# A causal window attention and a token/channel MLP mixer on one core: another planner table, transposed sums stored as they are, and softmax, u and stores planned apart

## The chip, the cores and the metric

The kernel runs on one core of a Trainium2 chip. The metric is the device time of one launch in microseconds (us). Beside it stands one execution that the hardware profiler recorded: its span, and what each engine did in it. Engines are called PE (matrix multiply; PEld is its weight load), DVE (vector), ACT (scalar), POOL and SP (the last two mostly issue transfers here).

## The reference

x is 8 batches of 4096 rows of 192 values, in float32. First each row becomes a weighted sum of itself and the six rows before it, with weights from a softmax over 7 taps for each of 8 heads of 24 values. Then an MLP over the rows of a batch (token mixing, 4096 to 256 to 4096) is added, and then an MLP over the values (channel mixing, 192 to 1536 to 192).

```
w = exp(wg - max(wg));  w = w / (sum(w) + 1e-9)                 # over the 7 taps
x[b, s, h] = sum over k of w[b, s, h, k] * x_pad[b, s + k, h]   # 24 values a head
u = x + (relu(x.T @ w_tok1) @ w_tok2).T                         # per batch, over 4096 rows
out = u + relu(u @ w_ch1) @ w_ch2
```

## The kernel before

The 32,768 rows are cut into 64 **chunks** of 512 rows (8 to a batch); chunk and group numbers below are the same 0 to 63. Products that must be near float32 are made as two or three fast matmuls on a high and a low part, so nearly every tile has a `_hi` and a `_lo` twin that ACT (cast) and DVE (subtraction) make.

The stages of a chunk:

- **attention**: for each tap k, DVE multiplies the chunk's rows by the weights (`product`, L203). Tap 0 goes to the sum `xa`; taps 1 to 6 each go to a buffer `pr` (4 of them) and are added to `xa` by a transfer that accumulates (L221, issued on POOL). The next addition to the same `xa` waits until the last has landed, and a `pr` buffer is free when its addition has landed. Chunks go in **pairs**, tap by tap: product for one, product for the other, and so on, so 12 additions a pair;
- **turn** (L285): DVE transposes `xa` in blocks of 32 by 32, ACT moves 24 blocks into place (L293), and two transfers on ACT's queue keep the result `xs` in DRAM (L275, L276). It comes back later as `xb` (L313, L314, on SP's queue);
- **token1** (L483, L484; `th`): PE multiplies `xa` by the first token weights and DVE adds the result to `h1s`. From the third batch on it takes `xh`, the high and low parts of `xa` (L257 on ACT, L260 on DVE). When all 8 chunks of a batch are through, `make_h1` gives `h1`;
- **token2** (L513; `up`): PE multiplies `h1` by the second token weights for chunk m; DVE adds `xb` (L520 to L522) and gives u; ACT and DVE make its parts (L524 to L529). token2 of a batch's first chunk needs `h1` of that batch, so the last token1 of the batch before it;
- **channel1** (`ph`, L544, L549) and **channel2** (`acc`, L567): for each group three rounds q = 0, 1, 2. channel1 of a round fills two `ph` tiles, ACT and DVE turn each into `h` (L552, L553), and channel2 of the round before follows on PE. A round's channel1 and channel2 together are called a **slot** here;
- **store**: DVE adds `acc` to u (L577 to L579), which also frees the only `acc` tile, and transposes twice (L581, L582); ACT moves 12 blocks (L589) into `out_tile`, and two transfers on ACT's queue write them out (L599).

A prologue makes chunks 0 to 7 (the first batch) in another way, on PE, and turns the int64-boxed weights into float32 (`convert`).

**The order.** Every engine takes its instructions in the order of the program, and the program's order is made by a planner written out in the kernel: PE's order is a loop over groups and rounds, in which one token1 or token2 fits after each slot. All other work stands in chains of items with a cost, and `pump` issues items, earliest start first, while they end before a limit. `at` holds the planned time of each engine. An item is "v" (DVE), "a", "s" or "u" (ACT), "n" or "t" (no cost; "t" only once its wait is over), "gate" (a condition) or "w" (a time to wait for). How long an addition takes to land is a constant of the plan:

```
ISSUE, ADD = 1000, 5000          # L606, ns
done[m] = on("pool", ISSUE, at["dve"] + HOP, done.get(m, 0.0)) + ADD     # L223
pr_free.append(done[m])                                                   # L224
yield "w", 0, lambda: pr_free.popleft()                                   # L232, ahead of a product
```

Nothing of the plan is checked at run time: an engine that comes to a product whose buffer is not free stands there, with all that follows it in its order. `need` (L697) is what the loop calls where PE cannot go on: it moves the planned time of PE on by 500 ns at a time until the condition holds.

Of the kernel before, what the change touches and what calls it, by code (L numbers as in the profile page):

```python
# [21 lines left out]
def mixer_kernel(ctx: ExitStack, tc: tile.TileContext, x, wg, wt1, wt2, wc1, wc2, out):  # L22
# [22 lines left out]
    TAPS = [(k,) for k in range(K)]  # L45
    PR = 4

# [115 lines left out]
    def softmax(m):  # L163
        t = wgt.pop(m)
        nt = SM * CT
        wn = p1.tile([P, K, nt, H], F32, tag="wn", name="wn")
# [4 lines left out]
        yield "v", 540, lambda: nc.vector.tensor_reduce(mx, t, axis=AX.X, op=ALU.max)  # L171
        yield "v", 540, lambda: nc.vector.tensor_sub(t, t, bc(mx))
        yield "a", 470, lambda: nc.scalar.activation(t, t, AF.Exp)
        yield "v", 540, lambda: nc.vector.tensor_reduce(mx, t, axis=AX.X, op=ALU.add)
# [5 lines left out]
        yield "v", 540, lambda: nc.vector.tensor_mul(wn.rearrange("p k t h -> p t h k"), t, bc(mx))  # L180
# [15 lines left out]
    def attention(ms):  # L196

        done, sums = {}, {}
        cost = 70 + CT * D * 1.05
# [8 lines left out]
        def one(m, k, first):  # L208
            t = new_xa(m) if k == 0 else late.tile([P, CT, D], F32, tag="pr", name="pr", bufs=PR)
            product(m, k, t)  # L210
            if first:
                sums[m] = t
            else:
                prt[m] = t

        def add_dve(m):
            nc.vector.tensor_add(sums[m], sums[m], prt.pop(m))
            pr_free.append(at["dve"])
# [7 lines left out]
        for ks in TAPS:  # L226
            for m in ms:
                for k in ks:
                    if k == 0:
                        yield "gate", 0, lambda m=m: xa_free(m)  # L230
                    else:
                        yield "w", 0, lambda: pr_free.popleft()  # L232
                    yield "v", cost, lambda m=m, k=k: one(m, k, k == ks[0])
                    if k != ks[0]:
                        yield "v", cost, lambda m=m: add_dve(m)
                if ks[0] != 0:
                    yield "n", 0, lambda m=m: add_dma(m)

        def summed(m):
            xa_at[m] = done[m]  # L240
            add_chain(two_parts(m), done[m])
            state["summed"] = m
        for m in ms:
# [7 lines left out]
    def two_parts(m):  # L251
# [9 lines left out]
        if m // NCH >= F1:  # L261
            yield "a", 760, hi
            yield "v", 876, lo
# [6 lines left out]
    Q = 32  # L270

    def keep(m, t):

        xst[m] = dram.tile([2, P, N], F32, name=f"xs{m}")
        nc.scalar.dma_start(xst[m][0], t[:, 0, :])  # L275
        nc.scalar.dma_start(xst[m][1, DC:P], t[DC:P, 1, :])  # L276

    def turns():

        for m in range(NCH, NG):  # L280
            box = {}

            def turn():
                box["t"] = late.tile([P, CT, D], F32, tag="t", name="t")
                nc.vector.transpose(box["t"].rearrange("p c d -> p (c d)"), xat[m].rearrange("p c d -> p (c d)"))  # L285
                box["s"] = late.tile([P, 2, N], F32, tag="ts", name="ts")
                state["turned"] = m

            def move(part):
                t = box["t"].rearrange("p c (d j) -> p c d j", j=Q)  # L290
                for d, n in part:
                    dst, to = (box["s"][:, 0], d * Q) if d < DA // Q else (box["s"][:, 1], DC + d * Q - DA)
                    nc.scalar.copy(dst[to:to + Q, :].rearrange("p (c n j) -> p c n j", c=CT, j=Q)[:, :, n, :],  # L293
                                   t[n * Q:(n + 1) * Q, :, d, :])
            yield "gate", 0, lambda: state["summed"] >= m
            yield "w", 0, lambda: xa_at[m]
            yield "v", 876, turn
            every = [(d, n) for d in range(D // Q) for n in range(P // Q)]
            for at_ in range(0, len(every), MOVES):
                part = every[at_:at_ + MOVES]  # L300
                yield "u", 300 * len(part), lambda part=part: move(part)

            def last():
                keep(m, box["s"])
                state["kept"] = m
                return max(at["act"], at["pe"]) + KEEP
            yield "w", 0, last

    def load_xt(m):

        xbt[m] = p1.tile([P, 2, N], F32, tag="xb", name="xb", bufs=2)
        s = xst.pop(m)
        nc.sync.dma_start(xbt[m][:, 0, :], s[0])  # L313
        nc.sync.dma_start(xbt[m][DC:P, 1, :], s[1, DC:P])  # L314
# [26 lines left out]
    def turn_first(m):  # L341
# [9 lines left out]
        nc.scalar.copy(t[:, 0, :], ps[:, 0, :])  # L351
        nc.scalar.copy(t[DC:P, 1, :], ps[DC:P, 1, :])
        if m >= 2:
            keep(m, t)
# [40 lines left out]
    def convert_w2(i):  # L395
# [5 lines left out]
        v = v.rearrange("p (k n c) -> p k n c", k=KR, c=CT)  # L401
        t = p1.tile([P, KR, 2, N], F32R, tag="w2", name="w2")
        hi, lo = (t[:, :, l].rearrange("p k (c n) -> p k n c", c=CT) for l in range(2))
# [3 lines left out]
        def last():  # L407
            state["vals"] -= 1
            w2t[i] = t
            nc.gpsimd.dma_start(s3[i], t.rearrange("p k l n -> p (k l n)").bitcast(F32))  # L410
        yield "n", 0, last

    def load_w2(m):
        t = p1.tile([P, KR, 2, N], F32R, tag="w2", name="w2")
        nc.sync.dma_start(t.rearrange("p k l n -> p (k l n)").bitcast(F32), s3[m % NCH])
# [90 lines left out]
    def token2(m):  # L506
# [3 lines left out]
        for n, steps in ((1, ((C_HL, 0), (C_HL, 1))), (0, ((A_HI, 0), (A_HI, 1), (A_LO, 0)))):  # L510
            for k in range(KR):
                for j, (d, l) in enumerate(steps):
                    nc.tensor.matmul(up[:, n, :], h1[:, k, d], w[:, k, l, :], start=k == 0 and j == 0,  # L513
# [5 lines left out]
        c = slice(0, DC)  # L519
        nc.vector.tensor_add(uc[c], up[DC:P, 1, :], xb[DC:P, 1, :])  # L520
        nc.vector.tensor_add(uc[c], up[c, 1, :], uc[c])
        nc.vector.tensor_add(ua, up[:, 0, :], xb[:, 0, :])  # L522
        a_hi, a_lo, c_hi, c_lo = (late.tile([P, N], F32R, tag=x, name=x, bufs=2) for x in ("a_hi", "a_lo", "c_hi", "c_lo"))
        nc.scalar.copy(c_hi[c], uc[c])  # L524
# [431 lines left out]
```

## Time and profile before

| what | value |
|---|---|
| time, 3 runs | 2341.88 us median (2335.44 to 2349.58) |
| profiled execution | 2351.83 us, span 2350.1 us |
| PE busy | 2188.0 us (93%) |
| DVE busy | 1624.9 us (69%) |
| ACT busy | 1405.7 us (60%), of it 397.5 us for the 1344 moves of L293 |
| POOL busy | 304.4 us, 336 additions issued |
| transfers | 429.65 MB, mean 183 GB/s |

How to read the rows: a group of instructions has busy time and mean duration, then the idle time of its engine just before them and what ended it. A row of waits has total us, how often, and the longest. In a timeline row the bracket holds the idle time ahead of the instruction and what ended it. A row of stretches gives busy time and count of each engine in a stretch, then the clock granted to PE (1.00 is full speed), the busy share of the 16 transfer engines, and GB/s. Matmuls overlap, so a PE row's mean duration is longer than the time from one matmul to the next.

### The profile page before, as it was taken

The page shows a single profiled execution, that of the slowest core. Times are in us where ns is not written, and L with a number is a line of the kernel's source. Part 1 is how long each engine was busy: PE and PEld are TensorE (multiplying, and loading weights), DVE is VectorE, ACT ScalarE, POOL GpSimd, SP SyncE. Part 2 cuts the span into 40 slices and gives each one's busy share as a digit, 9 for nine tenths or more (in the row PEclk, how much of TensorE's full clock was granted, in tenths as well). Part 3 has the DMA queues.
Part 4 walks back from the last instruction along what each step waited for, and adds up shares of the span by engine and source line. Part 5 has one row for each costly group of instructions (what it writes and reads, how often), then busy time and mean ns, then how long its engine had stood idle before and what let it go on. Part 6 is the DMA issues. An engine that isn't in the chain of part 4 may idle for free.

```text
span 2350.1 us, 28487 instructions
## 1 busy us (share of the span) xinstructions
PE 2188.0 (93%) x10464; PEld 1703.4 (72%) x10464; DVE 1624.9 (69%) x1932; ACT 1405.7 (60%) x2969; POOL 304.4 (13%) x359
## 2 busy tenths in 40 slices
PE   8968999899899999999999999999999999999998
PEld 5746777677677777777777777777777777777776
DVE  8886888686666767667777776676776667544443
ACT  5546786566666656665556766555666656544444
POOL 0011222111111111111111111111111111000000
PEclk9978999899999999999999999999999999999999
DMA  7677989896778787677887777778777777212210
GB/s 283 221 197 211 247 223 233 215 250 164 214 200 219 203 187 203 168 207 195 199 223 185 186 189 204 194 192 223 172 184 204 192 195 173 93 63 63 63 57 21
DMA packets 131820, 429.65 MB, mean 183 GB/s; under 512 B 16232, under 2 KB 26728, under 8 KB 116320
## 3 DMA queue, kind: packets, MB, share of 16 engines
q0 software_dynamic: 49536, 140.53, 31.6%
q1 hardware_dynamic: 58016, 237.74, 29.8%
q10 hardware_dynamic: 24128, 49.56, 8.0%
q8 instruction: 82, 1.34, 0.2%
q14 instruction: 58, 0.48, 0.1%
HBM read 225.13 MB, written 70.52 MB: 126 GB/s over the span
## 4 chain that ended last, share of the span: by engine, by line
PE 34%; DMA 29%; DVE 17%; ACT 14%; issue 4%; ACTq 1%; SPq 0%; POOLq 0%; DVEq 0%
DMA xa<-pr 24%; PE acc L567 13%; PE ph L544 8%; ACT ts L293 6%; DVE h L553 5%; PE ph L549 4%; ACT out_tile L589 4%; DVE pr L203 3%; PE tapsum L336 3%; PE up L513 2%; ACT h L552 2%; DMA xt<-in_x_dram 2%; DVE t L285 1%; DVE xa L203 1%; DMA val<-s 1%
## 5 line engine op out<-in xcount | busy, mean ns | idle before, releaser
L567 PE MATMUL acc<-h,w2s 128*128 128x512 f32 x3840 | 936.9, 399 | 34.4 <-DVE ua L579 34.3
L567 PEld LDWEIGHTS acc<-h,w2s 128*128 128x128 f32 x3840 | 713.9, 190 | 247.0 <-issue 88.6
L552 ACT ACTIVATE h<-ph 128x1024 fp32r<-128x1024 f32 x384 | 373.2, 1024 | 332.8 <-PE ph L549 312.5
L553 DVE SCALAR_TENSOR_TENSOR h<-ph,h 128x1024 fp32r<-128x1024 f32 x384 | 450.9, 1215 | 171.9 <-ACT h L552 171.9
L221 POOL DMA_DIRECT2D xa<-pr x336 | 292.7, 874 | 1554.7 <-DVE pr L203 806.7
L293 ACT COPY ts<-t 32x128 f32<-32x128 f32 x1344 | 397.5, 296 | 47.8 <-DMA xs<-ts 10.0
L203 DVE TENSOR_TENSOR pr<-xt,wn 128x768 f32<-128x768 f32 x336 | 310.0, 946 | 157.6 <-DMA xa<-pr 156.6
L544 PE MATMUL ph<-a_hi,w1a_hi 128*128 128x512 f32 x768 | 316.2, 412 | 71.7 <-DVE h L553 64.2
L544 PE MATMUL ph<-a_hi,w1a_lo 128*128 128x512 f32 x768 | 310.8, 405 | 0.0
L544 PE MATMUL ph<-a_lo,w1a_hi 128*128 128x512 f32 x768 | 310.5, 404 | 0.1
L544 PEld LDWEIGHTS ph<-a_hi,w1a_hi 128*128 128x128 f32 x768 | 151.2, 197 | 110.6 <-DVE h L553 71.2
L589 ACT COPY out_tile<-ua 32x256 f32<-32x256 f32 x512 | 206.8, 404 | 8.5 <-DVE ua L582 1.8
L513 PE MATMUL up<-w,h 128*128 128x512 f32 x640 | 161.7, 400 | 21.0 <-ACT w L404 10.6
L544 PEld LDWEIGHTS ph<-a_lo,w1a_hi 128*128 128x128 f32 x768 | 151.1, 197 | 34.1 <-DVE a_lo L527 1.2
L544 PEld LDWEIGHTS ph<-a_hi,w1a_lo 128*128 128x128 f32 x768 | 151.5, 197 | 30.1
L549 PE MATMUL ph<-c_hi,w1c_hi 64*128 64x512 f32 x768 | 172.7, 446 | 0.0
L513 PEld LDWEIGHTS up<-w,h 128*128 128x128 f32 x640 | 123.4, 193 | 48.5 <-ACT w L404 11.0
L549 PE MATMUL ph<-c_lo,w1c_hi 64*128 64x512 f32 x768 | 152.3, 393 | 0.0
L549 PE MATMUL ph<-c_hi,w1c_lo 64*128 64x512 f32 x768 | 151.4, 391 | 0.0
L520 DVE TENSOR_TENSOR uc<-up,xb 64x512 f32<-64x512 f32 x64 | 44.4, 693 | 130.7 <-ACT out_tile L589 103.4
L549 PEld LDWEIGHTS ph<-c_hi,w1c_hi 64*128 64x128 f32 x768 | 72.4, 185 | 78.5 <-issue 69.4
L483 PE MATMUL th<-xh,w 128*128 128x384 f32 x384 | 113.7, 360 | 10.5 <-ACT w L157 9.3
(77 smaller groups left out, 1963.4 us busy)
## 6 DMA issues: line engine op xcount, KB each, us to landing
xa<-pr POOLq DMA_DIRECT2D x336, 384.0 KB, 5.9
w<-s SPq DMA_DIRECT2D x96, 1024.0 KB, 6.3
xt<-in_x_dram SPq DMA_DIRECT2D x56, 960.0 KB, 9.2
out_dram<-out_tile ACTq DMA_DIRECT2D x128, 192.0 KB, 3.1
raw<-in_moe_w_tok_dram SPq DMA_DIRECT2D x16, 1024.0 KB, 6.6
xs<-ts ACTq DMA_DIRECT2D x62, 256.0 KB, 5.2
xb<-xs SPq DMA_DIRECT2D x62, 256.0 KB, 7.1
s<-w POOLq DMA_DIRECT2D x8, 1024.0 KB, 9.8
```

What stands on the lines that cost most here:

```text
L203: nc.vector.tensor_mul(t.rearrange("p t (h g) -> p (t h) g", h=H).rearrange("p (o n) g -> p o n g", o=1), x_k, w)
L221: nc.gpsimd.dma_start(xat[m].rearrange("p t d -> p (t d)"), sums[m].rearrange("p t d -> p (t d)"), accum_op=ALU.add)
L293: nc.scalar.copy(dst[to:to + Q, :].rearrange("p (c n j) -> p c n j", c=CT, j=Q)[:, :, n, :], t[n * Q:(n + 1) * Q, :, d, :])
L336: nc.tensor.matmul(ps[:, n, 0:half * D], ident, prs[k][:, n * half:(n + 1) * half, :], start=k == 0, stop=k == K - 1)
L483: nc.tensor.matmul(th[:, r, 0:2 * D], w[:, c, 0, rs], xh[:, c, :], start=c == 0, stop=False)
L513: nc.tensor.matmul(up[:, n, :], h1[:, k, d], w[:, k, l, :], start=k == 0 and j == 0, stop=k == KR - 1 and j == len(steps) - 1)
L544: nc.tensor.matmul(ph[p][:, j, :], w[:, fs], u, start=n == 0, stop=False)
L549: nc.tensor.matmul(ph[p][:, j, :], w[rows, p * P:(p + 1) * P], u[rows], start=False, stop=n == 2)
L552: nc.scalar.activation(h[:, :, 0, :], ph[p], AF.Relu)
L553: nc.vector.scalar_tensor_tensor(h[:, :, 1, :], ph[p], 0.0, h[:, :, 0, :].bitcast(F32), op0=ALU.max, op1=ALU.subtract)
L567: nc.tensor.matmul(acc[:, n, :], w2s[:, f, d], h[:, j, l, :], start=f == 0 and i == 0, stop=f == NF - 1 and i == len(steps) - 1, skip_grou ...
L589: nc.scalar.copy(dst, src[to:to + Q].rearrange("p (c n k d) -> p c n k d", c=CT, n=2, d=Q)[:, :, n])
```

## The change: what it does

**Plan numbers.** ISSUE and ADD go from 1000 and 5000 to 900 and 7000, LOAD (a load's landing) from 5000 to 8000; the costs of the other items move by some per cent. The tap table gets a second form (two taps summed on DVE), used from chunk EARLY * 8 on; EARLY is 8, so from chunk 64, which does not exist. Every pair keeps its 12 additions.

**Turn.** The 24 ACT moves and the two stores on ACT's queue for each of 56 chunks go. DVE's transpose writes its blocks in another order, one transfer on SP's queue stores the tile as it is (128 rows of 3072 bytes), and the load puts the 32-row strips in place with six transfers of 32 rows in pieces of 512 bytes. Columns of u are then in another order, and the second token weights and the last moves follow it.

**Items of their own.** softmax becomes a chain of its own, one pair ahead of the products, with two `wn` tiles. The parts of u are no longer issued with token2 but are items (`u_parts`). The output transfers become "t" items on SP's queue. token2 makes the 128-row half first. `need` may name chains that go first.

```diff
+    TAPS = [(0,), (1, 2), (3, 4), (5, 6)]
+    TAPS0 = [(k,) for k in range(K)]
...
-        for ks in TAPS:
+        for ks in (TAPS if ms[0] >= EARLY * NCH else TAPS0):
...
             def turn():
-                box["t"] = late.tile([P, CT, D], F32, tag="t", name="t")
-                nc.vector.transpose(box["t"].rearrange("p c d -> p (c d)"), xat[m].rearrange("p c d -> p (c d)"))
-                box["s"] = late.tile([P, 2, N], F32, tag="ts", name="ts")
+                t = box["t"] = late.tile([P, D // Q, CT * Q], F32, tag="t", name="t")
+                nc.vector.transpose(t.rearrange("p d (c b) -> p d c b", c=CT),
+                                    xat[m].rearrange("p c (d a) -> p d c a", a=Q))
                 state["turned"] = m
 
-            def move(part):
-                t = box["t"].rearrange("p c (d j) -> p c d j", j=Q)
-                for d, n in part:
...
+            def keep():
+                xst[m] = dram.tile([P, D // Q, CT * Q], F32, name=f"xs{m}")
+                nc.sync.dma_start(xst[m], box["t"])
+                state["kept"] = m
...
+        for d in range(D // Q):
+            dst = t[d * Q:(d + 1) * Q, 0] if d < DA // Q else t[DC + d * Q - DA:DC + (d + 1) * Q - DA, 1]
+            nc.sync.dma_start(dst.rearrange("a (n j) -> a n j", n=P // Q),
+                              s[:, d, :].rearrange("(n a) j -> a n j", a=Q))
...
-        for n, steps in ((1, ((C_HL, 0), (C_HL, 1))), (0, ((A_HI, 0), (A_HI, 1), (A_LO, 0)))):
+        for n, steps in ((0, ((A_HI, 0), (A_HI, 1), (A_LO, 0))), (1, ((C_HL, 0), (C_HL, 1)))):
...
+        yield "u", 620, lambda: nc.scalar.copy(a_hi, ua)
+        yield "u", 620, lambda: nc.scalar.copy(c_hi[c], uc[c])
+        yield "v", 610, lambda: nc.vector.tensor_sub(a_lo, ua, a_hi.bitcast(F32))
+        yield "v", 610, lambda: nc.vector.tensor_sub(c_lo[c], uc[c], c_hi[c].bitcast(F32))
+        yield "u", 620, lambda: nc.scalar.copy(c_hi[e], uc[c])
+        yield "u", 620, lambda: nc.scalar.copy(c_lo[e], c_lo[c].bitcast(F32))
...
-                nc.scalar.dma_start(rows.rearrange("(k p c) d -> p k (c d)", k=OB, c=CT),
+                nc.sync.dma_start(rows.rearrange("(k p c) d -> p k (c d)", k=OB, c=CT),
...
-        yield "n", 0, last
+        yield "n", 0, moved
+        yield "t", 0, last
...
-    ISSUE, ADD = 1000, 5000
+    ISSUE, ADD = 900, 7000
...
-    LOAD = 5000
-    KEEP = 3000
+    LOAD = 8000
...
-    TOP, LOW = 1040, 1235
+    TOP, LOW = 1000, 1180
...
-            for c in chains[2:] + chains[1::-1]:
+            urgent = [c for c in chains if c.key in keys and not c.blocked() and c.item is not None]
+            for c in urgent or chains[3:] + chains[2:0:-1] + chains[:1]:
...
+    def softmaxes():
+
+        for m in range(NCH, NG, SM):
+            yield "gate", 0, lambda: m - SM in soft_at and state["done"] >= m - SM - 1 or m == NCH
+            yield "w", 0, lambda: wg_at.get(m, 0.0)
+            yield from softmax(m)
...
+        soft = softmaxes()
+        run(islice(soft, 2, 9))
         run(w2_it)
...
-                need(token1_ready)
+                need(token1_ready, ("w1", state["token1"] + 1), ("x", state["token1"] + 1))
                 do_token1()
-            need(lambda: g + 1 in w2t and g + 1 in xbt and state["stored"] >= g - 1)
+            need(lambda: g + 1 in w2t and g + 1 in xbt and state["stored"] >= g - 1, (convert_w2, g + 1), ("o", g - 1))
             do_token2(g + 1)
```

**What moves.** DVE in the middle of the program, at the end of a pair's products (`pr`), where `h` is the eviction that PE waits for. Before:

```order
L203 TENSOR_TENSOR pr<-xt,wn 128x768
L553 SCALAR_TENSOR_TENSOR h<-ph,h 128x2x512 x2
L203 TENSOR_TENSOR pr<-xt,wn 128x768 x3
L520 TENSOR_TENSOR uc<-up,xb 64x512
L521 TENSOR_TENSOR uc<-up,uc 64x512
L522 TENSOR_TENSOR ua<-up,xb 128x512
L525 TENSOR_TENSOR c_lo<-uc,c_hi 64x512
L527 TENSOR_TENSOR a_lo<-ua,a_hi 128x512
L203 TENSOR_TENSOR pr<-xt,wn 128x768 x2
L553 SCALAR_TENSOR_TENSOR h<-ph,h 128x2x512 x2
```

and now:

```order
L207 TENSOR_TENSOR pr<-xt,wn 128x768
L589 STREAM_TRANSPOSE ua<-ua 128x512
L207 TENSOR_TENSOR pr<-xt,wn 128x768
L560 SCALAR_TENSOR_TENSOR h<-ph,h 128x2x512 x2
L207 TENSOR_TENSOR pr<-xt,wn 128x768 x2
L175 TENSOR_REDUCE mx<-wg 128x64
L176 TENSOR_TENSOR wg<-wg,mx 128x448
L518 TENSOR_TENSOR ua<-up,xb 128x512
L519 TENSOR_TENSOR uc<-up,xb 64x512
L520 TENSOR_TENSOR uc<-up,uc 64x512
L560 SCALAR_TENSOR_TENSOR h<-ph,h 128x2x512 x2
```

Of a pair's 12 `pr` products the last five stood between two evictions; now two do, and the evictions from the first four products to the last are three instead of two.

ACT in the same part of the program, between evictions (`out_tile` are the moves of the store, `ts` those of the turn). Before:

```order
L552 ACTIVATE h<-ph 128x2x512 x2
L589 COPY out_tile<-uc 32x4x2x32 x2
L589 COPY out_tile<-ua 32x4x2x32 x4
L599 DMA out_dram<-out_tile 32x2x768 x2
L293 COPY ts<-t 32x4x32 x10
L275 DMA xs_8650<-ts 128x512
L276 DMA xs_8650<-ts 64x512
L524 CAST c_hi<-uc 64x512
L526 CAST a_hi<-ua 128x512
L528 CAST c_hi<-uc 64x512
L529 CAST c_lo<-c_lo 64x512
```

and now:

```order
L559 ACTIVATE h<-ph 128x2x512 x2
L596 COPY out_tile<-uc 32x8x32 x2
L596 COPY out_tile<-ua 32x8x32 x4
L559 ACTIVATE h<-ph 128x2x512 x2
L527 CAST a_hi<-ua 128x512
L528 CAST c_hi<-uc 64x512
L531 CAST c_hi<-uc 64x512
L532 CAST c_lo<-c_lo 64x512
L559 ACTIVATE h<-ph 128x2x512 x4
```

No transfer is issued on ACT any more in this part, and the parts of u stand behind an eviction, not before it.

PE where the second batch's first token2 stands. Before:

```order
L549 MATMUL ph<-c_lo,w1c_hi 128x512 x2
L567 MATMUL acc<-h,w2s 128x512 x20
L513 MATMUL up<-w_2772,h_2644 128x512 x10
L544 MATMUL ph<-a_hi,w1a_hi 128x512
L544 MATMUL ph<-a_hi,w1a_lo 128x512
```

and now:

```order
L556 MATMUL ph<-c_lo,w1c_hi 128x512 x2
L574 MATMUL acc<-h,w2s 128x512 x20
L499 MATMUL th<-xa,val 128x192 x16
L511 MATMUL up<-w_2458,h_2794 128x512 x10
L551 MATMUL ph<-a_hi,w1a_hi 128x512
```

Two token1 (8 matmuls each), this token2 and the channel1 that takes its u now follow each other with nothing between; before, the batch's last token1 lay earlier and a slot lay between token2 and its channel1. The third batch's first token2 stands in the same way. Later batches have their last token1 two slots ahead.

More of the change, by code (lines that the diff above doesn't have):

```diff
@@ L681, in pump @@
                     start = max(at["act"], c.wait)
-                    if kind == "s" and scalar or not state["late"] and (start > now + 400 or start + c.item[1] > end):
+                    if kind == "s" and scalar > 1 or not state["late"] and (start > now + 400 or start + c.item[1] > end):
                         continue
@@ L838, in mixer_kernel @@
         pass
+    run(u_parts(0))
+    free["u"] = 0.0
     load_xt(2)
[L840 to L842 removed]
+    att = attentions()
+    run(last)
+    run(c2_it)
+    run(islice(att, FIRST))
+    chains[0:0] = [Chain(att), Chain(turns()), Chain(soft)]
     add_chain(load_w1(NCH))
```

187 lines of the change are left out of this document (93 added, 94 removed).

## The prediction

> **What bounds the kernel now.** I read the page's first parts, then the busy time by stretch, PE's timeline, the waits, and the additions. PE is busy 93% of the span, so it is the engine whose stalls are the time:
>
> ```profile
> PE 2188.0 (93%) x10464; PEld 1703.4 (72%) x10464; DVE 1624.9 (69%) x1932; ACT 1405.7 (60%) x2969; POOL 304.4 (13%) x359
> PEclk9978999899999999999999999999999999999999
> DMA xa<-pr 24%; PE acc L567 13%; PE ph L544 8%; ACT ts L293 6%; DVE h L553 5%; PE ph L549 4%; ACT out_tile L589 4%; DVE pr L203 3%; PE tapsum L336 3%; PE up L513 2%; ACT h L552 2%; DMA xt<-in_x_dram 2%; DVE t L285 1%; DVE xa L203 1%; DMA val<-s 1%
> ```
>
> Yet the chain that ended last runs longest through the landing of additions (24%), and the clock row falls below full speed here and there. How long a group takes when nothing stalls is read from the starts of token2 on PE:
>
> ```profile
> 1723.96 2.43 PE L513 MATMUL up<-w,h 128*128 128x512 f32 x10
> 1755.70 2.43 PE L513 MATMUL up<-w,h 128*128 128x512 f32 x10
> ...
> 1791.61 1.75 PE L513 MATMUL up<-w,h 128*128 128x512 f32 x7
> ...
> 2060.04 1.29 PE L513 MATMUL up<-w,h 128*128 128x512 f32 x5
> ...
> 2089.49 1.75 PE L513 MATMUL up<-w,h 128*128 128x512 f32 x7
> ```
>
> 29.45 us without a token1 (2060.04 to 2089.49), 31.74 with one (1723.96 to 1755.70), so a token1 is 2.29. The group after that took 35.91. Next, the stretches between the first token2, the 17th, the 54th and the end; then the same stretches for token2 (10 matmuls each) and token1 (16 each) alone:
>
> ```profile
> 0.00:124.60 124.60, 109.93 (x480) 78.86 (x480) 105.45 (x84) 67.88 (x85) 3.50 (x10) 1.00 0.75 254
> 124.60:723.00 598.40, 530.55 (x2481) 411.95 (x2482) 458.79 (x551) 390.77 (x833) 105.20 (x124) 0.93 0.83 214
> 723.00:1995.10 1272.10, 1204.93 (x5847) 946.65 (x5846) 898.26 (x1108) 782.51 (x1753) 195.72 (x225) 0.98 0.77 195
> 1995.10:2350.10 355.00, 342.60 (x1659) 265.91 (x1657) 162.45 (x191) 164.53 (x300) 0.00 (x0) 0.99 0.20 60
> ...
> 723.00:1995.10 1272.10, 89.83 (x370) 69.42 (x370) 0.98 0.77 195
> ...
> 124.60:723.00 598.40, 46.34 (x272) 44.12 (x272) 12.64 (x23) 1.42 (x3) 0.93 0.83 214
> 723.00:1995.10 1272.10, 89.29 (x592) 87.49 (x592) 38.60 (x70) 1.92 (x4) 0.98 0.77 195
> ```
>
> Middle: 37 groups, 37 token1, floor 37 x 31.74 = 1174, taken 1272: **98 us lost**. Early: 16 groups and 17 token1, 16 x 29.45 + 17 x 2.29 = 510, less some 14 as the first two groups hold five slots instead of six and one channel2 less: floor about 496, taken 598: **102 us lost**. After 1995 nothing is to be had: groups run at 29.45. So the most that any change of order can bring is some 200 us.
>
> Who makes PE wait in the middle stretch, and who makes those wait:
>
> ```profile
> PE ph L544 <- DVE h L553: 36.0, 14, 3.7
> PE acc L567 <- DVE ua L579: 31.1, 16, 3.6
> DVE pr L203 <- DMA xa<-pr: 137.2, 56, 8.2
> DVE t L285 <- DMA xa<-pr: 48.3, 15, 4.1
> ```
>
> PE waits 67 us, always for DVE; DVE stands 185 us for landings of additions, with evictions behind it. One such place:
>
> ```profile
> 1700.94 0.96 DVE L203 TENSOR_TENSOR pr<-xt,wn 128x768 f32<-128x768 f32 x1 [7.11 <-DMA xa<-pr]
> ...
> 1703.09 0.79 PE L544 MATMUL ph<-a_hi,w1a_hi 128*128 128x512 f32 x1 [2.87 <-DVE h L553]
> ...
> 1703.00:1706.50 3.50, 3.41 (x8) 2.73 (x9) 2.82 (x5) 0.58 (x1) 0.87 (x1) 0.50 0.91 175
> ```
>
> A product stands 7.11 us for a buffer, the eviction behind it is late, PE idles 2.87, and then its clock is 0.50 for the next 3.5 us. So a stall is paid twice; the 98 us are 67 of waiting and about 31 of half clock.
>
> The Trainium skill, "TensorE: Matmul & The Clock Gate", section "HAM oscillation — how this bites in real kernels", gives as its rule that idle gaps over about 3.4 us are to be avoided. By it a gap of 2 to 3 us would cost its own length and no more. The rows differ: 2.87 us were enough for 3.5 us at half clock, so here the measurement decides.
>
> **The change part by part.** *The planned landing.* An addition was planned at 1.0 + 5.0 = 6.0 us from issue to landing, now at 0.9 + 7.0 = 7.9. What it takes:
>
> ```profile
> DMA to landing us min/median/max: 3.9/5.9/13.6
> ...
> 1737.93 1.76 POOL L221 DMA_DIRECT2D xa<-pr  x2 [29.71 <-DVE pr L203]
> 1746.52 0.87 POOL L221 DMA_DIRECT2D xa<-pr  x1 [6.83 <-DMA xa<-pr]
> ...
> 1764.24 0.88 POOL L221 DMA_DIRECT2D xa<-pr  x1 [4.62 <-DMA xa<-pr]
> 1770.12 0.87 POOL L221 DMA_DIRECT2D xa<-pr  x1 [5.00 <-DMA xa<-pr]
> ```
>
> The median is near the old number, but a late one delays all later ones of its chunk. Four rounds took 1764.24 - 1737.93 = 26.3 us, 6.6 each: 2.3 us over the old plan, 5.3 under the new. So DVE, which now meets the product later, finds the buffer free in a pair like this. In the order, three evictions now lie between the first four products and the last two. With a slot at (29.45 - 2.29) / 3 = 9.1 us (11.3 with a token), the last product comes some 34 us after the first, when the fourth round must have landed: 26 to 29 us at 6.6 to 7.3 a round. The turn and the parts of xa come two evictions later, at some 52 us, against 6 x 7 = 42 for the last landing. Slack everywhere, 4 to 10 us; it is gone at 9 us a round. Bounds for the middle stretch: 0 (every wait comes back at another place) and 98 (none does). I take two thirds, **-65**, nearer to none, since 6.6 lies well under 9, but loads collide with single rounds.
>
> What is late next is DVE itself: 898 us in 37 groups is 24.3 us a group of 31.74, so it has 7 us to spare, unevenly: a slot with store, two products for `xa`, turn and parts is fuller than its 11.3 us by about a microsecond, which the token matmul after it covers.
>
> *The turn.* ACT's moves and its transfers:
>
> ```profile
> L293 ACT COPY ts<-t 32x128 f32<-32x128 f32 x1344 | 397.5, 296 | 47.8 <-DMA xs<-ts 10.0
> ...
> 1727.74 0.35 ACTq L275 DMA_DIRECT2D xs<-ts  x1
> 1729.23 0.45 ACTq L276 DMA_DIRECT2D xs<-ts  x1
> 1755.42 0.34 ACTq L599 DMA_DIRECT2D out_dram<-out_tile  x1
> ```
>
> 24 x 0.296 + 0.35 + 0.45 + 2 x 0.34 = 8.6 us of ACT a group go. ACT is busy 782 of 1272, 21 us a group, and PE waits for DVE; so in the middle this is worth nothing by itself. It shortens casts that sit behind moves, and in the early stretch, where weights are converted, it frees ACT: 391 of 598 busy. That is inside the terms. The transpose is one instruction as before.
>
> *The transfers.* The loads become six of 64 KB instead of two:
>
> ```profile
> w<-s SPq DMA_DIRECT2D x96, 1024.0 KB, 6.3
> xs<-ts ACTq DMA_DIRECT2D x62, 256.0 KB, 5.2
> xb<-xs SPq DMA_DIRECT2D x62, 256.0 KB, 7.1
> ...
> SPq L415 <- PE up L513: 1054.9, 52, 25.1
> ```
>
> SP issues per group 1 (turn) + 2 (out) + 4 (more loads) = 7 more, at 0.35 to 0.45 us some 3 us; it already stands 1055 us waiting for token2 alone, so the time is there. The price of 512-byte pieces is not in the trace: from nothing (same bytes) to twice the 7.1 us of today's landing. Behind it, with xb loaded nearly two groups (60 us) ahead, 14 us is still hidden: 0. Should that cover go, DVE would stand before u and the same 2.9 + 1.7 us a stall would be due. The SP wait that is added (a store waits for DVE's transpose or ACT's moves) has the weight loads behind it; token2's next weights have a group's 31.74 us for 6.3.
>
> *The early stretch.* Group 1 begins:
>
> ```profile
> 174.02 0.79 PE L513 MATMUL up<-w,h 128*128 128x512 f32 x1 [10.58 <-ACT w L404]
> ...
> 182.77 0.53 PE L544 MATMUL ph<-a_hi,w1a_hi 128*128 128x512 f32 x1 [2.75 <-ACT a_hi L526]
> ```
>
> PE stands 10.58 us for a converted weight whose conversion lay behind products and another conversion; now it goes first. Bounds 0 and -13.3 (both waits); I take **-10**. Of the 89 us of loss left there, DVE's stands for landings and a crowded ACT make a part; bounds 0 and -89, I take 0.4 of it, **-35**, less than in the middle since conversions stay. Against that, PE's order now has token1, token2 and channel1 in a row at two batch starts. Each pays twice a wait like the 2.75 above (for h1, for u's parts), 5.5, and some 3.5 at half clock, up to 14.5 as group 1 did; I take 10 each, **+20**. The stretch: -25.
>
> *The prologue.* The softmax of the ninth and tenth chunk moves ahead of the first token2: its exponential on ACT and six short DVE operations, bounds 0 and 4 us; **+1**, as ACT takes one more instruction there. The tail after the last matmul is the same.
>
> *The sum*, against the profiled execution's own 2351.83 (span 2350.1, 1.7 around it): -65 - 25 + 1 = **-89**, 2263. That execution was 10 us above the median of the runs, so for the median 2342 - 89 = **2253 us**.
>
> **The rivals.** *The waits move (half).* Loads of 1 MB and two x tiles collide with single rounds, and DVE stands at other products. For it: landings reach 13.6, and the transfer engines are 77% busy and will be busier with shorter groups. Against it: 5.3 us of slack in four rounds. A third of the middle and -6 early: about -39, **2303**.
>
> *Near the floor.* No landing is met late, the half clock goes too, the two batch starts cost little: -90 in the middle, -55 early, +1: **2196**. For it: no other engine is near full. Against it: PE waits in early groups for conversions that remain.
>
> *Slower: additions beyond the plan.* token1 now stands at a fixed place right after its pair's additions, while PE takes nothing else. If a round takes r us, the sixth has landed at 6r, and token1 comes at some 56; from r = 9 PE waits 6 (r - 9) for each of 28 pairs, and 1.7 at half clock. At r = 9.2 that is (1.2 + 1.7) x 28 = +81; the middle's -65 then fails too, and -24 remains of the rest: +57, **2399**. It decides from r = 9 on. For it: single rounds of 8.6 (1737.93 to 1746.52). Against it: the four rounds averaged 6.6.
>
> The Trainium skill, "DMA: Bandwidth & Descriptors", section "Queues, rings and completion order", says that each transfer engine goes round the queue rows that have work, a packet at a time. By it, emptying ACT's row leaves the additions' row a larger turn, not a smaller one, which speaks against this rival; no row here shows the turns, and I give it 0.07 rather than 0.10 for that.
>
> *No change.* The loss goes from landings to DVE's full slots and the two batch starts: **2342**.
>
> **How the numbers follow.** Chances: forecast 0.53, half 0.22, near the floor 0.13, no change 0.05, slower 0.07. What a measurement of this kernel can tell from no change is about 0.5%, 12 us. Faster 0.53 + 0.22 + 0.13 = 0.88, same 0.05, slower 0.07. The range that holds 8 in 10 goes from the near-floor case to just over the half case, 2196 to 2315: it leaves out half of the near-floor case (0.06), no change and slower (0.12). The bounds of the unknown pieces (early -89, middle -98) would reach lower, about 2145, which needs all at once.
>
> **What would show it.** In the changed profile: DVE's stands for landings (185 us in the middle) down to some 60, PE's for h and ua from 67 to some 25; groups in the middle alternating no longer between 31.7 and 36, but near 32.5; the clock there 0.99 or more; a gap of 5 to 15 us on PE at the first token2 of the second and the third batch; ACT's busy time down by 397 us, which by itself moves nothing. It would be wrong if DVE stands as long at turn or parts as it did at products, if a wait for `xb` or token weights shows on PE or DVE, or if token1 waits for `xh`.

## The result, and the profile after

The changed kernel takes **2256.48 us** (median of 4 runs, 2251.6 to 2258.84); the kernel before took 2345.73 beside it. The ratio is 0.961, 95% interval 0.956 to 0.967. Its profiled execution took 2258.16 us (span 2256.3), 93.7 less than the profiled execution before (2351.83). Forecast were 2253 and a difference of 89.

From the page of the changed kernel, the busy times:

```profile
PE 2162.9 (96%) x10464; PEld 1686.6 (75%) x10464; DVE 1618.1 (72%) x1932; ACT 1010.6 (45%) x1625; POOL 300.7 (13%) x359
```

ACT is down by 395 us, and PE by 25, which fits matmuls that no longer run at half clock. The stretches of the prediction, cut again at the first, the 17th and the 54th token2 (columns as in the prediction: length, busy PE, PEld, DVE, ACT, POOL, clock, share of transfer engines, GB/s), and the same for token1 alone (16 matmuls each):

```profile
0.00:125.30 125.30, 109.77 (x480) 78.83 (x480) 108.78 (x90) 68.38 (x86) 3.49 (x10) 1.00 0.76 253
125.30:711.50 586.20, 532.81 (x2509) 413.01 (x2509) 441.53 (x527) 266.54 (x403) 94.66 (x113) 0.95 0.80 203
711.50:1900.60 1189.10, 1175.69 (x5803) 926.51 (x5804) 893.13 (x1112) 521.60 (x873) 192.21 (x224) 0.99 0.86 211
1900.60:2256.30 355.70, 344.62 (x1675) 268.28 (x1673) 174.62 (x207) 154.04 (x264) 10.31 (x12) 0.99 0.30 77
...
125.30:711.50 586.20, 46.22 (x256) 0.95 0.80 203
711.50:1900.60 1189.10, 92.26 (x592) 0.99 0.86 211
```

The floors are made as in the prediction: 29.45 us a group, 2.29 a token1, 14 off in the early stretch. One thing differs: the change has a slot more ahead of the 17th token2 and a slot less behind it. Without token1, PE has 2509 - 256 = 2253 matmuls in the early stretch, where it had 2481 - 272 = 2209, so 44 more; in the middle it has 44 fewer (5803 for 5847, token1 alike); and a slot is 24 matmuls of channel1 and 20 of channel2. At 9.1 us a slot: early, 16 groups, 256/16 = 16 token1 and the slot, floor 503, taken 586, so **83 us lost** (102 before); middle, 37 groups and 592/16 = 37 token1 less the slot, floor 1165, taken 1189, **24 us lost** (98 before). All 24 lie before 950 us; after that every group takes the floor, as two starts of token2 show (PE's timeline):

```profile
1233.98 2.43 PE L511 MATMUL up<-w,h 128*128 128x512 f32 x10
1265.72 2.43 PE L511 MATMUL up<-w,h 128*128 128x512 f32 x10
```

So 74 us came out of the middle and 19 out of the early stretch. Who waits in the middle (711.5 to 1900.6; total, times, longest), DVE first, then PE:

```profile
DVE pr L207 <- DMA xa<-pr: 76.7, 42, 4.1
DVE t L285 <- DMA xs<-t: 14.1, 3, 6.3
...
PE ph L551 <- DVE h L560: 5.2, 2, 5.0
PE th L481 <- DMA w<-s: 3.1, 1, 3.1
PE th L481 <- issue: 2.3, 1, 2.3
PE up L511 <- ACT h L467: 1.8, 1, 1.8
PE ph L551 <- ACT a_hi L527: 1.4, 1, 1.4
```

DVE still stands 77 us at products, but never over 4.1 us (8.2 before), and PE's waits are 15 us in all. After 948 us PE does not wait at all, though most of DVE's stands at products lie there (948.3 to 1900.6):

```profile
DVE pr L207 <- DMA xa<-pr: 60.6, 32, 4.1
```
In the early stretch PE still waits 53 us; the largest:

```profile
PE ph L551 <- ACT a_hi L527: 12.5, 4, 4.3
PE ph L551 <- DVE h L560: 11.6, 2, 6.4
PE th L499 <- DMA val<-s: 11.6, 1, 11.6
PE th L482 <- DVE w L162: 5.0, 1, 5.0
```

The 11.6 us are new. They stand ahead of the second batch's first token2, where the last token1 waits for its weights `val`. PE's timeline, then SP's and DVE's at the same time:

```profile
409.76 2.11 PE L499 MATMUL th<-xa,val 128*128 128x192 f32 x12
423.44 5.46 PE L499 MATMUL th<-xa,val 128*128 128x192 f32 x16 [11.57 <-DMA val<-s]
...
410.50 8.00 SPq L291 DMA_DIRECT2D xs<-t  x2
418.55 0.95 SPq L370 DMA_DIRECT2D val<-s  x2
...
417.17 0.98 DVE L285 STREAM_TRANSPOSE t<-xa 128x768 f32<-128x768 f32 x1 [3.45 <-DMA xs<-t]
```

SP spends 8 us on two stores of transposed sums, the second of which must wait for DVE's transpose; the load of the weights is issued only behind them. The transpose for its part stands 3.45 us for the first store, as there is one tile `t`.

### The profile page after: what moved, and what is told of

Its sections match the earlier page's. It is cut to its first block, busy times and chain, and to the rows that moved or that the text cites. A ratio compares the mean times of both kernels' runs of the same rounds, so it can differ in the third digit from the quotient of the medians.

```text
span 2256.3 us, 27414 instructions
## 1 busy us (share of the span) xinstructions
PE 2162.9 (96%) x10464; PEld 1686.6 (75%) x10464; DVE 1618.1 (72%) x1932; ACT 1010.6 (45%) x1625; POOL 300.7 (13%) x359
## 4 chain that ended last, share of the span: by engine, by line
PE 81%; DMA 8%; DVE 6%; ACT 3%; issue 1%; SPq 0%; POOL 0%; ACTq 0%; DVEq 0%; POOLq 0%
PE acc L574 34%; PE ph L551 20%; PE ph L556 12%; PE up L511 5%; DMA xa<-pr 5%; PE tapsum L331 3%; PE th L481 3%; ACT out_tile L596 1%; PE th L499 1%; PE th L482 1%; DVE h L560 1%; DMA xs<-t 1%; DMA w<-s 1%; ACT h L559 1%; DVE pr L207 1%
## 5 line engine op out<-in xcount | busy, mean ns | idle before, releaser
L574 PE MATMUL acc<-h,w2s 128*128 128x512 f32 x3840 | 926.4, 395 | 2.2 <-DVE ua L586 2.2
L574 PEld LDWEIGHTS acc<-h,w2s 128*128 128x128 f32 x3840 | 706.2, 188 | 210.7 <-issue 68.6
L551 PE MATMUL ph<-a_hi,w1a_hi 128*128 128x512 f32 x768 | 308.0, 401 | 30.7 <-DVE h L560 16.8
L551 PE MATMUL ph<-a_lo,w1a_hi 128*128 128x512 f32 x768 | 305.4, 398 | 2.7 <-DVE a_lo L529 2.6
L551 PE MATMUL ph<-a_hi,w1a_lo 128*128 128x512 f32 x768 | 304.9, 397 | 0.0
L596 ACT COPY out_tile<-uc 32x256 f32<-32x256 f32 x256 | 103.3, 403 | 16.5 <-DVE uc L588 11.9
L482 PE MATMUL th<-xh,w 128*128 128x192 f32 x384 | 98.2, 256 | 5.0 <-DVE w L162 5.0
```

Source lines behind the costliest of these rows:

```text
L482: nc.tensor.matmul(th[:, r, 0:D], w[:, c, 1, rs], xh[:, c, 0:D], start=False, stop=c == CT - 1)
L551: nc.tensor.matmul(ph[p][:, j, :], w[:, fs], u, start=n == 0, stop=False)
L574: nc.tensor.matmul(acc[:, n, :], w2s[:, f, d], h[:, j, l, :], start=f == 0 and i == 0, stop=f == NF - 1 and i == len(steps) - 1, skip_grou ...
L596: nc.scalar.copy(dst, src[to:to + Q].rearrange("p (n e d) -> p n e d", n=2, d=Q)[:, n])
```

## The experiments

Each kernel was timed in three rounds (the last in five) beside the kernel before, which took 2338 to 2348 us in them; ratios are therefore sharper than times. Losses are from each profiled execution, with the floors above, and with its own token1: 16 early (17 in the kernel before, 18 in e3), 36 to 39 in the middle. e1, e3, e5 and e11 have their slots as the kernel before, the others as the change.

| kernel | us | ratio to before (95%) | lost early | lost in the middle |
|---|---|---|---|---|
| before | 2346 | 1 | 102 | 98 |
| the change | 2256 | 0.961 (0.956-0.967) | 83 | 24 |
| e1 change, old landing | 2375 | 1.012 (1.009-1.014) | 105 | 104 |
| e2 landing alone (7.9) | 2229 | 0.949 (0.945-0.952) | 65 | 11 |
| e3 turn alone | 2420 | 1.029 (1.026-1.033) | 98 | 172 |
| e4 change, val ahead | 2248 | 0.957 (0.953-0.960) | 76 | 18 |
| e5 turn and landing | 2239 | 0.958 (0.955-0.960) | 78 | 13 |
| e6 landing 6.9 | 2283 | 0.977 (0.974-0.980) | 94 | 38 |
| e7 landing, conversions earlier | 2246 | 0.961 (0.959-0.963) | 89 | 6 |
| e8 landing 8.9 | 2304 | 0.986 (0.983-0.989) | 118 | 36 |
| e9 change, weights timed | 2255 | 0.962 (0.957-0.967) | 67 | 35 |
| e10 e9, val ahead, early 6.9 | 2242 | 0.956 (0.951-0.960) | 52 | 40 |
| e11 e5 with big loads | 2237 | 0.953 (0.949-0.958) | 75 | 12 |
| e12 e10, two t tiles | 2207 | 0.941 (0.938-0.944) | 45 | 11 |

**e1 and e2: the landing taken out, and the landing alone.** The same line, in the changed kernel and in the kernel before:

```diff
-    ISSUE, ADD = 900, 7000        # e1, in the changed kernel
+    ISSUE, ADD = 1000, 5000
...
-    ISSUE, ADD = 1000, 5000       # e2, in the kernel before
+    ISSUE, ADD = 900, 7000
```

> The changed kernel with one line put back: an addition is planned at 1.0 + 5.0 us again. Theory (the planned landing carries the gain in the middle): DVE comes to the products too early again, its waits for landings rise from 99 us to 140 or more, PE's waits and half clock return between the 23rd and the 57th token2, where no loss was left, and most of the 83 us gained there go: 2315 us (2295 to 2340). Rival (ACT without the moves, and the items of their own, carry it): 2250 to 2265 us, no loss between the 23rd and the 57th token2.

> The kernel before with one line changed: an addition is planned at 0.9 + 7.0 us. Theory (the planned landing carries the gain in the middle): groups in the middle fall from 34.4 us to 32.5 or less, 2346 - 60 = 2285 us (2265 to 2305). Rival (the landing does nothing while ACT still makes 24 moves a chunk, or the wait moves to turn and parts): 2330 to 2355 us.

The theory held, further than expected: both times lie beyond the theory's ranges (2295 to 2340 and 2265 to 2305). Without the planned landing the rest of the change is 1.2% slower than before; the landing alone is faster than the whole change. In microseconds: the landing takes 118 off the kernel before (2347 to 2229) and 119 off the rest of the change (2375 to 2256); the rest adds 28 and 28. Taken whole, the two add up; a part of the rest, the turn, does not (e3 and e5). (The 83 us that the expectation names are 74 by the floors above.) In the middle of e1 (725 to 1990 us) DVE no longer stands at products (42 us) but at the turn, ACT at the cast for token1 with evictions behind it, and PE pays:

```profile
DVE t L285 <- DMA xa<-pr: 94.4, 19, 10.9
DVE t L285 <- DMA xs<-t: 83.2, 17, 6.9
...
DVE pr L207 <- DMA xa<-pr: 42.0, 39, 4.2
...
PE ph L556 <- ACT c_hi L531: 54.9, 17, 10.0
...
ACT xh L262 <- DMA xa<-pr: 131.9, 19, 14.6
```

In e2's middle the landings are hardly ever met late:

```profile
DVE pr L203 <- DMA xa<-pr: 14.8, 10, 2.4
```

**e3: the turn alone.** In the kernel before, the 24 moves go, the store and the six loads come, with the order of columns that they need; the plan's other numbers and its order rules stay.

```diff
-            yield "v", 876, turn
-            every = [(d, n) for d in range(D // Q) for n in range(P // Q)]
...
-                yield "u", 300 * len(part), lambda part=part: move(part)
...
+            yield "v", 890, turn
+            yield "t", 0, keep
```

> The kernel before with the turn alone: ACT's 24 moves go, the store is one transfer on SP, the load six; the columns of u, token2's weights and the last moves follow; the plan's numbers and the order of the rest stay. Theory (the forecast: ACT's relief is worth nothing by itself in the middle): groups in the middle stay at 34 us, some us less in the early stretch, 2336 us (2325 to 2345). Rival (ACT's 8.6 us a group were what made evictions late): 2300 us or less.

Both missed: it is 2.9% **slower**. The order shows why. The turns are one chain, in which the 24 moves of a chunk stood ahead of the next chunk's transpose, so that the transposes of a pair, and what came behind them, lay late in DVE's order, by when more of the additions had landed in spite of the short plan. Without the moves the planner packs closer: in the order of most pairs of the middle, one pair of evictions lies between a pair's last product and its first transpose, where there were two, and two ahead of its second, where there were three. DVE now stands 137 us at the transpose in the middle (48 before) and 128 at products (137). Waits of the middle (to 2040 us), then one such place in DVE's timeline, with two evictions behind it and PE idle 6.46 us for them:

```profile
DVE t L285 <- DMA xa<-pr: 136.6, 18, 11.1
DVE pr L203 <- DMA xa<-pr: 128.4, 73, 9.8
...
1099.70 0.61 DVE L174 TENSOR_REDUCE mx<-wg 128x64 f32<-128x448 f32 x1
1110.92 0.98 DVE L285 STREAM_TRANSPOSE t<-xa 128x768 f32<-128x768 f32 x1 [10.61 <-DMA xa<-pr]
...
1113.36 2.34 DVE L549 SCALAR_TENSOR_TENSOR h<-ph,h 128x1024 fp32r<-128x1024 f32 x2
```

**e5 and e11: turn and landing together, and the turn without small pieces.** e5 is e3 with e2's line. e11 loads the sums back in two transfers; it leaves out that the 32-row strips are put in place, so its u is made from sums in a wrong order:

```diff
-        for d in range(D // Q):
-            dst = ...
-            nc.sync.dma_start(dst.rearrange("a (n j) -> a n j", n=P // Q),
-                              s[:, d, :].rearrange("(n a) j -> a n j", a=Q))
+        nc.sync.dma_start(t[:, 0, :], s[:, 0:4, :].rearrange("p d j -> p (d j)"))
+        nc.sync.dma_start(t[DC:P, 1, :], s[DC:P, 2:6, :].rearrange("p d j -> p (d j)"))
```

> The kernel before with two parts of the change: the plan of 0.9 + 7.0 us an addition and the turn (stores as they are on SP's queue, six loads). The landing alone gave 2229 us, the whole change 2256. Theory (the turn costs the 28 us that lie between: SP's queue waits for DVE's transposes with weight loads behind it, and the small loads make additions land later): 2250 us (2240 to 2265). Rival (with the landing planned the turn is free, and softmax, u and stores as items of their own cost the 28): 2228 us (2220 to 2236).

> The kernel before with the landing of 0.9 + 7.0 and the turn, but the turned sums are loaded back by two transfers of 2048-byte rows instead of six in pieces of 512 bytes. Left out: the strips are not put in place, so u is made from the sums in a wrong order; bytes, instructions and the plan stay the same. Theory (the small pieces make the additions land later, 7.0 us in the median against 5.8 with the landing alone, and that is the turn's price): median landing 6.0 or less, DVE's stands for landings at products from 99 to 40 us or less, 2228 us (2222 to 2233). Rival (it is the stores on SP's queue that hold the loads behind them): landing stays near 7, 2236 to 2242 us.

e5 lies between its two answers. By the profiled spans the landing alone is 2225.3, with the turn 2240.1, the whole change 2256.3: the turn costs 15 of the 31 us, softmax, u and stores as own items with the other numbers 16; by the ratios (0.949, 0.958, 0.961) it is rather three quarters and one quarter, so the split is rough. With the turn, additions land later and DVE meets them late; e5's transfers and waits, beside those of e2 (whole span):

```profile
xa<-pr POOLq DMA_DIRECT2D x336, 384.0 KB, 7.0
...
DVE pr L203 <- DMA xa<-pr: 99.1, 70, 4.1
DVE t L285 <- DMA xs<-t: 27.5, 11, 3.8
```

```profile
xa<-pr POOLq DMA_DIRECT2D x336, 384.0 KB, 5.8
...
DVE pr L203 <- DMA xa<-pr: 20.6, 13, 4.1
```

It is not the small pieces, which was e11's theory: it has none, and shows the same landing and the same stands.

```profile
xa<-pr POOLq DMA_DIRECT2D x336, 384.0 KB, 6.9
...
DVE pr L203 <- DMA xa<-pr: 97.8, 70, 4.2
```

The queue's share of the transfer engines falls only from 36.2 to 34.7%, and the time from 2239 to 2237, inside the intervals. The Trainium skill, "DMA: Bandwidth & Descriptors", section "Specifications", gives 512 bytes as the piece from which a transfer runs at full rate. The traces of the two runs do not quite bear that out: on SP's queue a packet of 512 bytes took 32.9 ns in the mean (e5), one of 2048 bytes 97.4 (e11), so 15.6 against 21.0 bytes a ns; these loads are 22 of 430 MB, too little for it to show in the time.

Nor are the late landings most of what the turn costs. Of the 99 us that e5's DVE stands for them, 90 lie in the middle, where e5 loses 2 us more than e2 (13 against 11). The other 13 of the 15 us lie in the early stretch, where PE waits longer for u's parts, at one place 9.1 us (e5, then e2):

```profile
PE ph L540 <- ACT a_hi L522: 18.9, 4, 9.1
...
PE ph L544 <- ACT a_hi L526: 8.6, 3, 3.0
```

What puts the part of u late there was not separated. Why additions land later with the turn stays open: their moment against other loads has shifted, but which load meets them was not separated, and that the stores on SP's queue do it (e11's rival) is not shown either. Stores on a queue other than SP's were not tried.

**e6 and e8: the plan at 6.9 and at 8.9.**

```diff
-    ISSUE, ADD = 1000, 5000
+    ISSUE, ADD = 900, 6000        # e6; e8 has 900, 8000
```

> The kernel before with an addition planned at 0.9 + 6.0 us. The old number (6.0) gave 2346 us, 7.9 gave 2229; a round takes about 7 us in the traces, just over this plan's 6.9. Theory (what counts is how far the plan lies below the measured round, so this is most of the way): 2255 us (2240 to 2280). Rival A (a plan below the measured round pays in full): 2320 us or more. Rival B (the early stretch gains from shorter plans, and the middle has slack enough): 2225 us or less.

> The kernel before with an addition planned at 0.9 + 8.0 us. Theory (beyond the measured round, more planned time only makes sums and token1 later, at the starts of batches above all): 2245 us (2233 to 2265). Rival (single late landings still cost at 7.9): 2222 us or less.

Planned at 6.0, 6.9, 7.9 and 8.9 us, an addition gives 2346, 2283, 2229 and 2304. e6 came out just above its theory's range. e8 lost more than expected (2304 for at most 2265), in another place than e6: sums and token1 come late by the plan itself, and PE stands where batches begin. PE's waits from the first token2 to the 25th:

```profile
PE th L483 <- DVE xh L260: 23.4, 4, 8.7
PE up L513 <- DVE h L471: 19.3, 3, 14.0
```

The best of the four is about a microsecond over a round (6.6 us in the prediction's four), and the way down on both sides costs 50 to 75 us.

**e4: the second batch's weights one chunk ahead.**

```diff
-        if m + 1 < NG:
-            add_chain(load_w1(m + 1), key=("w1", m + 1))
+        while state["w1"] < min(m + (2 if state["vals"] == 0 and not state["jobs"] and m + 2 < F1 * NCH else 1), NG - 1):
+            state["w1"] += 1
+            add_chain(load_w1(state["w1"]), key=("w1", state["w1"]))
```

> The changed kernel with the token-1 weights loaded one chunk further ahead in the second batch, once the weight conversions are through. Theory (the 11.57 us that PE stands ahead of the second batch's first token2 are a load that waits on SP's queue behind the store of the transposed sums): that gap and the 13.6 us of half clock behind it go, 11.6 + 6.8 = 18 us: 2238 us (2232 to 2246). Rival (the next thing is as late: the sum itself, h1, the parts of u): 2250 to 2260 us, with a gap of 5 us or more at the same place.

Half of it: the wait for `val` is gone, and the next thing, h1, is late by 5.49 us in its place; 9 us are gained instead of 18, and the intervals of the two ratios touch.

```profile
413.22 2.84 PE L499 MATMUL th<-xa,val 128*128 128x192 f32 x16 [1.00 <-issue]
421.54 4.64 PE L511 MATMUL up<-w,h 128*128 128x512 f32 x10 [5.49 <-ACT h L467]
```

**e7: conversions earlier.** In e2, two ACT steps of a conversion may be issued in one call:

```diff
-                    if kind == "s" and scalar or not state["late"] and ...
+                    if kind == "s" and scalar > 1 or not state["late"] and ...
```

> The kernel before with 0.9 + 7.0 us an addition and one more number: two ACT steps of a weight conversion may be issued in one call of the planner, not one (as in the changed kernel). Theory (the 9 us that PE stands for group 1's converted weights go, and half clock behind them): 2215 us (2208 to 2222). Rival (the start of the second batch takes them back, since its last sums set it): 2224 to 2234 us.

Missed: 17 us slower than e2. PE's wait ahead of group 1 falls only from 9.07 to 4.50 us, and the shifted order puts four token1 of the third batch where their weights have not been split yet (second batch to third, 425 to 716 us):

```profile
PE th L484 <- DVE w L158: 21.0, 4, 6.1
```

**e9, e10, e12: what was left.** The plan takes token1's weights for ready once they are issued. e9 gives them a time; e10 adds e4's edit and plans 0.9 + 6.0 for chunks 8 to 15; e12 adds a second `t` tile.

```diff
+                w1_at[m] = max(at["pe"], at["dve"]) + LOAD
...
+        w1_at[m] = at["dve"] + HOP if b == F1 else max(at["pe"], at["dve"]) + LOAD
...
-        return ready and ready[0][0] in w1t and ready[0][1] <= at["pe"] + 100
+        return ready and ready[0][0] in w1t and max(ready[0][1], w1_at[ready[0][0]]) <= at["pe"] + 100
...
-            done[m] = on("pool", ISSUE, at["dve"] + HOP, done.get(m, 0.0)) + ADD
+            done[m] = on("pool", ISSUE, at["dve"] + HOP, done.get(m, 0.0)) + (ADD if m >= 16 else 6000)   # e10
...
-                t = box["t"] = late.tile([P, D // Q, CT * Q], F32, tag="t", name="t")
+                t = box["t"] = late.tile([P, D // Q, CT * Q], F32, tag="t", name="t", bufs=2)   # e12
```

> The changed kernel with one more time in the plan: token1 is placed only when its weights are there (a load's 8 us after its issue, or the end of the split), not as soon as they are issued. Theory (what the change still loses before the 23rd token2 are weights that the plan takes for ready: 11.6 us for val at the second batch's start, 5.0 and 3.1 us for w in the third, each with 3.4 us or more at half clock): 2232 us (2222 to 2242), without those three gaps. Rival (the time only moves to later sums and token1 at the starts of batches): 2250 to 2262 us.

> The same, and the second batch's token-1 weights one chunk further ahead, and an addition of chunks 8 to 15 planned at 0.9 + 6.0 us instead of 7.0. Theory (in the second batch the sums set when token1 can start, so a shorter plan there brings the second token2 start forward, and DVE has room for the landings met late): 2215 us (2205 to 2230), the first token2 of the second batch at 410 or before (430.1 in the changed kernel). Rival (as in the kernel with 6.0 planned for all chunks, evictions are late behind products): 2235 us or more.

> The kernel of the run before last (weights timed in the plan, second batch at 6.0) with a second t tile, for which the 512 bytes of the prologue's identity are given back after it. Theory (what was won in the early stretch there was lost again because DVE's transpose stands for the store of the tile before, 139 us in all, with evictions behind it): those stands go, groups from the 24th token2 on run at 31.7 us, 2220 us (2210 to 2230), below the 2229 of the landing alone. Rival (the stands move to the products, and the plan of this version is too full): 2236 us or more.

e9 missed: the waits for `w` go, but `val` (9.6 us) stays, since the load still stands behind the stores on SP's queue, and most of what the early stretch gains (83 to 67) the middle loses (24 to 35). e10 missed too: its second batch starts at 414 us (430 in the change), and the early loss is 52, but the middle's is 40. What e10's rival put on products lies at the transposes, by DVE's waits there:

```profile
DVE t L285 <- DMA xs<-t: 109.6, 17, 7.6
DVE h L562 <- ACT h L561: 76.9, 51, 6.8
DVE pr L207 <- DMA xa<-pr: 28.9, 21, 3.6
```

A transpose waits for the store of the tile before, which waits on SP. With a second tile no transpose of DVE waits for a store, and the middle loses 11 us instead of 40; e12's two stretches:

```profile
124.20:671.70 547.50, 524.18 (x2508) 408.49 (x2509) 448.11 (x537) 266.49 (x404) 98.36 (x116) 0.97 0.87 222
671.70:1848.00 1176.30, 1168.18 (x5804) 922.34 (x5804) 902.55 (x1114) 522.54 (x872) 202.34 (x233) 1.00 0.88 216
```

e12 takes 2206.6 us (2204.7 to 2210.5), below its theory's range, 1% under e2 and 2% under the change. It is the fastest of the kernels.

## Why the prediction was right, and where it was not

The time was right (2256 against 2253), and so were its two large terms, within 9 us each. That the sum came within 3 us is in part luck, since the two errors have opposite signs; and one error hid in the sum, that most parts of the change cost time.

- **What bounds the kernel**: right. The two losses, 102 and 98 us, are what every kernel of the table moves, and the landings of additions, which held the longest share of the chain, were the cause of the middle's (e1, e2).
- **The planned landing, -65 in the middle**: right in the main, a little small. It is -74 in the change and -87 alone (e2), so the term that was mis-sized is "I take two thirds". Its reason, "slack everywhere", held only in part: buffers were not free at every product. DVE's stands for landings fell from 185 to 77 us (forecast 60), with 14 for stores beside them. What counts is that the stands became short: after 948 us there are 32, of at most 4.1 us, and none makes PE wait; in the kernel before, one of 7.11 us cost PE 2.87. PE's waits fell from 67 to 15 us (forecast 25), the clock rose to 0.99 as forecast, and groups take 32.1 us in the mean (forecast 32.5), 31.74 each from the 23rd token2 on.
- **The early stretch, -25**: it gave 19. Against the floors, the first two groups lost 33 us and now 25, so -9 (forecast -10): PE's wait for group 1's weights fell from 10.58 to 0.47 us, but the one for u's part behind it rose from 2.75 to 4.25. The two batch starts were put at +20 and cost 15 more than before: from the 8th to the 10th token2 62.1 + 24.8 us for a floor of 65.8, from the 16th to the 18th 47.7 + 26.2 for 63.5, so 32 us lost where the same groups had lost 16 (the last 5 of the 15 fall in the middle stretch). The rest is the term that was too large: it was put at -35 and gave -21; with the landing alone (e2) the same groups gave the 35. At the batch starts the forecast had PE wait for h1 and u's parts; at the second batch it waited 11.57 for token weights, at the third 1.79 for h1 and 2.08 for u's parts.
- **The transfers, 0**: the step that failed is the sentence on the SP wait. It said that the loads behind a store are hidden since token2's next weights have a group's time. Behind the same store stood token1's weights, and two token1 in a row leave them no time. The forecast had named a wait for token weights on PE as a sign that it was wrong, and this one came. For the six loads themselves 0 was right, also for their pieces (e11).
- **The turn, "worth nothing by itself"**: wrong in sign. Alone it costs 73 us (e3), beside the landing 10 by the times and 15 by the spans (e5). Alone, the relief of an engine that is not the bound changed the planner's order, and the old order had covered a part of what the short plan left open.
- **Prologue, +1**: the first token2 is at 125.3, after 124.6.
- **The rivals**: "half" did not come; "near the floor", 2196 (its own terms, -90 - 55 + 1, give 2198), was not reached by the change, but e12 is within 11 us of it. "Slower, additions beyond the plan" did not come: token1 waited for no sum in the middle. It comes in e8, though by a plan too long, not by rounds too slow.

What the forecast missed as a whole is that the change would have been faster without most of its parts: the landing alone takes 2229 us.

## What to carry to other kernels

Where an order is planned by constants, measure the constants first: one line was worth 118 us, all the rest together cost 28, and in this kernel a plan of 1 us less or more than the best cost 50 to 75 us. Work taken off an engine that is not the bound still moves the order, so time it apart from the rest. And for each wait put on a shared queue, list everything behind it, not only the transfer that one has in mind.

## What the runs showed of the hardware

Not every idle gap of PE near 1.8 us is followed by half clock. After the 1.8 us ahead of the third batch's first token2 the clock of the next 3.7 us was 0.54; after the 1.8 us at 586 us (`acc` for `ua`) it was 1.00. Stretches of the changed kernel (the clock is the third number from the end):

```profile
712.00:715.70 3.70, 3.51 (x9) 2.25 (x8) 0.25 (x2) 0.00 (x0) 0.85 (x1) 0.54 1.07 178
719.00:722.60 3.60, 3.60 (x11) 2.38 (x11) 0.04 (x1) 0.62 (x1) 0.00 (x0) 0.53 1.03 317
586.40:590.00 3.60, 3.56 (x16) 2.96 (x17) 3.57 (x5) 2.83 (x8) 1.57 (x2) 1.00 0.98 177
```

The second row follows two gaps of 1.43 and 0.65 us. So here one gap of 1.79 us, and one of 1.43 with 0.65 behind it, each cost some 1.7 us more (3.7 x 0.46 and 3.6 x 0.47), and one of 1.77 cost nothing more; what decides it, the runs do not show.
